# SSM parameters taken 128 channels at a time beside the units, half-height generator products, and a different opening

## The chip, the cores and the metric

The kernel runs on one core of a Trainium2 chip. A core has four engines that compute, each with its own instruction stream: TensorE (PE; its weight loads are listed as PEld), VectorE (DVE), ScalarE (ACT) and GpSimd (POOL). A fifth, SyncE (SP), issues nearly all DMAs here, one after the other in a fixed order. An engine works through its instructions in the order in which they were written and waits on semaphores for the others. The metric is the device time of one execution in microseconds (us). The kernel before took 719.56 us (median of three executions, 719.55 to 720.75).

## The reference

The input `x` is 2048 tokens of 640 channels. Two branches are mixed by a gate per token:

```
x = A_u
g = sigmoid((x * gate_w).sum(-1, keepdims=True))
a = S4D(x)                     # a long convolution per channel, plus u * D_skip
b = relu(x @ w1) @ w2          # 640 -> 1728 -> 640
out = g * a + (1 - g) * b

# S4D, per channel d, with N = 128 states:
dt = exp(log_dt);  A = -exp(log_A_real) + 1j * A_imag
C  = (C_real + 1j * C_imag) * dt[:, None]
P  = exp((A * dt[:, None])[:, :, None] * pos)      # 640 x 128 x 2048
K  = 2 * real(einsum("dn,dnl->dl", C, P))          # the taps, 640 x 2048
y  = irfft(rfft(u, 4096) * rfft(K, 4096))[:2048] + u * D_skip
```

## The kernel before, in words

The work has three strands, which share the engines.

**Feed-forward** (`feed_forward`). The 2048 tokens are 8 groups of 256, the 1728 hidden channels 14 blocks of 128, taken in three parts of 5, 5 and 4 blocks (`PARTS`). One group and one part are a unit: 75 matrix products for the hidden layer and 60 for the second layer (60 and 48 in the last part). Every operand is split into a high and a low half in a rounded 32-bit format, so each product is made three times (names `xh`, `xl`, `w1h`, `w1l`, `hh`, `hl`; output `pf`). In part 0 each group's input is transposed on TensorE (`pk<-ident,xs`), split by ScalarE and VectorE, and stored for the later parts.

**Parameters and taps** (`params`, `ssm`). `params` (L612 on) takes `log_A_real`, `A_imag`, `C_real`, `C_imag` and `log_dt` and makes, per channel and state, a phase step in turns, a decay exponent, the size of C and its angle. It does so with chains of VectorE steps on tiles of all 640 channels, 128 partitions by 5 x 128 columns: an exponential by polynomial (`exp_`, 13 steps), two reciprocals (five steps each), an arctangent and a square root on ScalarE, and some twenty steps that put the angle in the right octant. The results are split in high and low halves (`hl`) and written to a scratch in DRAM (`ps`), from which they are read back (`PS`) so that the eight rows of 16 channels lie over the 128 partitions.
`ssm` then makes the taps 16 channels at a time, 40 times. `phases(c)` multiplies the rows by a constant table `tg` on TensorE (`pg`, two products of 512 columns), ScalarE rounds (`cs<-pg`) and VectorE subtracts (`sn<-pg,cs`). `exponents(c)` makes decays the same way (`px`, two products; `pe`, one), ScalarE takes exponentials and sines, GpSimd scales by C (`cm`). `factors(c)` is five VectorE products (`G`, `mg`, `cs`, `sn`). For every two such pieces, `taps(p)` runs 128 small products (`pk`), VectorE turns the result (`kt`), GpSimd adds `D_skip`, and SP stores it (`kd`).

**Convolution** (`conv`). Five blocks of 128 channels, each a two-stage transform of the taps and of the input, a product in between and the two stages back: `stage1` (`pc<-ck,tf` and `pc<-ut,tf`), `stage2` (`pc<-vk,tm`, `pc<-va,tm`), `inv2` (`pc<-t,tn`), `relay` (VectorE transposes), `inv1` (`pc<-vk,tw`). `start` closes the memory of the taps and opens that of the convolution. The results meet the feed-forward sums there (`yj`) or in `feed_forward` (`with_y`, `with_last`).

**What sets the order.** Nothing is reordered on the chip. A planner (`Plan`) is given every piece of work as a task with its engine, an estimated duration, its dependences, the buffers it takes (rings) and a rank. It runs a model of the engines and, whenever an engine is free, writes out the ready task of lowest rank; the instruction streams have that order. All operations go through one helper, which is why nearly every row of the profile has the line L228: rows are told apart by the names of their tiles. In `params` every task has a rank of 3 or 4 behind the feed-forward tasks' 0, the loads of the parameters come after the last weights of part 0, and the memory of the parameters (`prm`) must be closed (`prm_shut`) before any phase product may start:

```
        opened = self.prm_shut = A('PY', 'open', 0, go, self.params())
        a = visit[c, 1] = A('PE', None, 0.5, pe, [rd, opened, *self.tg_done], take=[p_], use=[r_], rank=2, mode='f')
```

Of the kernel before, what the change touches and what calls it, by code (L numbers as in the profile page):

```python
# [10 lines left out]
F32 = mybir.dt.float32  # L11
# [13 lines left out]
BEHIND = 3  # L25
# [11 lines left out]
def tables():  # L37
# [23 lines left out]

    pt, mg, me = np.zeros((16, 8, 16, 64)), np.zeros((16, 8, 16, 64)), np.zeros((16, 8, 16, 32))
# [3 lines left out]
    tg = np.concatenate([x.reshape(128, -1) for x in (pt, mg, me)], axis=1)  # L66
# [183 lines left out]
class Kernel:  # L250
    def __init__(self, tc, ctx, io, out):
# [7 lines left out]
        self.sc = dict(kd=T([64, D, 32], "kd"), ps=[T([1, 128, 8, 128], "ps0"), T([NT - 1, 128, 8, 128], "ps1")],  # L259
# [18 lines left out]
    def feed_forward(self):  # L278
# [117 lines left out]
        def hidden(p, g, i, fs):  # L396
# [41 lines left out]
            a = A('ACT', 'ff', 0.12 + 0.2 * len(fs), high, ts, take=[h_], use=[b_], rank=0)  # L438
            b = A('DVE', 'ff', 0.08 + 0.27 * len(fs), low, [a], use=[b_, h_], rank=0)
            H[p, g, i] = (a, b), h_  # L440

        def sums(p, g, j, q_, qld):
# [35 lines left out]
            for k in range(0, 3 * n, 4 if j == 0 else 5):  # L478
# [6 lines left out]
                  use=[b_] if p == 0 and j == 0 else [b_, q_], rank=0)  # L485
# [61 lines left out]
        self.zst, self.x_read = [], []  # L547
        xs = {0: load_x(0)}
# [8 lines left out]
        for p, n in enumerate(PARTS):  # L557
            if p == 1:
                gates()
            for g in range(8):  # L560
# [11 lines left out]
                for k, i in enumerate(range(0, n, 2)):  # L572
                    hidden(p, g, i, range(i, min(i + 2, n)))
                    if nxt[0] == 0:
                        trans(g + 1, k, xs[g + 1])
                        if k == 2 and g < 6:
                            xs[g + 2] = load_x(g + 2)
# [11 lines left out]
                for t in range(2):  # L589
                    es = [sums(p, g, j, q_, mx[t]) for j in (2 * t, 2 * t + 1)]  # L590
# [21 lines left out]
    def params(self):  # L612
        tc, nc, io, A = self.tc, self.nc, self.io, self.plan.add
        V, S, D_ = self.V, self.S, self.D
        tl, last = {}, {}


        def step(eng, dur, fn, kb=0, ch='c', deps=()):
            last[ch] = [A(eng, 'prm' + ch, dur, fn, [*last[ch], *deps], kb=kb, rank=dict(a=4, c=3)[ch])]
            return last[ch][0]  # L620

        def start():
            pp = tl['pp'] = self.prm
            T = lambda n, d=F32: pp.tile([128, NT, 128], d, name=n)
            tl['dt'] = pp.tile([128, NT], F32, name="dt")
            D_.dma_start(tl['dt'], io['A_log_dt'].rearrange("(t p) -> p t", p=128))
            for k, n in (('la', "A_log_A_real"), ('ai', "A_A_imag"), ('cr', "A_C_real"), ('ci', "A_C_imag")):
                tl[k] = T(f"ld_{n}")
                D_.dma_start(tl[k], io[n].rearrange("(t p) n -> p t n", p=128))
            for n in ("th", "ac", "as", "mx", "mn", "r", "s", "ph", "ra", "sa"):  # L630
                tl[n] = T(n)
            tl['ni'] = T("ni", I32)
        self.prm_load = A('SP', 'prm', 3.1, start, kb=1300, rank=0)
        last.update(a=[self.prm_load], c=[self.prm_load])

# [5 lines left out]

        def split(r, src, ch):
            def high():
                tl['hl', r] = tl['pp'].tile([128, NT, 2, 128], F32R, name=f"hl{r}")
                S.copy(tl['hl', r][:, :, 0], tl[src])
            step('ACT', 0.75, high, ch=ch)
            step('DVE', 0.85, lambda: V.tensor_sub(tl['hl', r][:, :, 1], tl[src], tl['hl', r][:, :, 0].bitcast(F32)), ch=ch)
            for k, ts in enumerate((slice(0, 1), slice(1, NT))):
                rs = (4, 6) if r == 4 else (r,)

                def store(k=k, ts=ts, rs=rs):
                    for x in rs:
                        D_.dma_start(self.sc['ps'][k].rearrange("t p k n -> p t k n")[:, :, x:x + 2],
                                     tl['hl', r][:, ts].bitcast(F32))
                self.rows_st[k].append(A('SP', 'prm', 0.62 * len(rs), store, last[ch], kb=128 * (1, NT - 1)[k] * len(rs),
                                         rank=1))
        self.rows_st = [], []

        def exp_dt(V):
            small = [tl['pp'].tile([128, NT], d, name=f"sm{i}") for i, d in enumerate((I32, F32, F32))]  # L660
            exp_(V, tl['dt'], *small)
        steps(13, 0.18, exp_dt, 'a')
        dt = last['a']
        steps(13, 0.68, lambda V: exp_(V, tl['la'], tl['ni'], tl['ra'], tl['sa']), 'a')

        def scaled(V):
            for t in range(NT):
                d = tl['dt'][:, t:t + 1]
                V.tensor_scalar(tl['th'][:, t], tl['ai'][:, t], d, 1.0 / TWO_PI, op0=ALU.mult, op1=ALU.mult)
            for t in range(NT):  # L670
                d = tl['dt'][:, t:t + 1]
                V.tensor_scalar(tl['la'][:, t], tl['la'][:, t], d, -1.0, op0=ALU.mult, op1=ALU.mult)
        steps(2 * NT, 0.2, scaled, 'a')
        th = last['a']
        split(0, 'th', 'a')
        split(4, 'la', 'a')
        T_ = lambda: (tl[k] for k in ('ac', 'as', 'cr', 'ci', 'mx', 'mn', 'r', 's', 'ph', 'th', 'ni'))
        W = lambda f: (lambda: f(*T_()))
        R = lambda f: (lambda V: f(V, *T_()))

        step('ACT', 1.5, W(lambda ac, as_, cr, ci, *o: (S.activation(ac, cr, AF.Abs), S.activation(as_, ci, AF.Abs))))
        steps(3, 0.7, R(lambda V, ac, as_, cr, ci, mx, mn, r, *o: (
            V.tensor_tensor(mx, ac, as_, op=ALU.max), V.tensor_tensor(mn, ac, as_, op=ALU.min),
            V.tensor_scalar(r, mx, 1e-37, None, op0=ALU.max))))
        for t in range(NT):
            steps(1, 0.85, R(lambda V, ac, as_, cr, ci, mx, mn, r, s, *o, t=t: V.reciprocal(s[:, t], r[:, t])))
        steps(1, 0.75, R(lambda V, ac, as_, cr, ci, mx, mn, r, s, *o: V.tensor_mul(r, mn, s)))
        step('ACT', 2.8, W(lambda ac, as_, cr, ci, mx, mn, r, s, ph, *o: (
            S.activation(ph, r, AF.Arctan), S.activation(r, r, AF.Square))))
        steps(1, 0.45, R(lambda V, ac, as_, cr, ci, mx, mn, r, *o: V.tensor_scalar(r, r, 1.0, None, op0=ALU.add)))  # L690
        step('ACT', 2.1, W(lambda ac, as_, cr, ci, mx, mn, r, s, *o: S.activation(s, r, AF.Sqrt)))
        for t in range(NT):
            steps(1, 0.85, R(lambda V, ac, as_, cr, ci, mx, mn, r, s, *o, t=t: V.reciprocal(mn[:, t], s[:, t])))
        steps(3, 0.8, R(lambda V, ac, as_, cr, ci, mx, mn, r, s, *o: (
            V.tensor_mul(r, r, mn), V.tensor_add(s, s, r), V.tensor_mul(mx, mx, s))))

        def by_dt(V):
            for t in range(NT):
                V.tensor_scalar(tl['mx'][:, t], tl['mx'][:, t], tl['dt'][:, t:t + 1], None, op0=ALU.mult)
        steps(NT, 0.22, by_dt, deps=dt)  # L700
        steps(1, 0.45, R(lambda V, ac, as_, cr, ci, mx, mn, r, s, ph, *o: V.tensor_scalar(ph, ph, 1.0 / TWO_PI, None,
                                                                                         op0=ALU.mult)))
        for cond, two, turn in ((ALU.is_gt, True, 0.25), (ALU.is_lt, False, 0.5)):
            steps(4, 0.65, R(lambda V, ac, as_, cr, ci, mx, mn, r, s, ph, *o, cond=cond, two=two, turn=turn: (
                V.tensor_tensor(mn, as_, ac, op=cond) if two else V.tensor_scalar(mn, cr, 0.0, None, op0=cond),
                V.tensor_scalar(r, ph, -2.0, turn, op0=ALU.mult, op1=ALU.add),
                V.tensor_mul(r, r, mn), V.tensor_add(ph, ph, r))))
        steps(3, 0.6, R(lambda V, ac, as_, cr, ci, mx, mn, r, s, ph, *o: (
            V.tensor_scalar(mn, ci, 0.0, None, op0=ALU.is_lt),
            V.tensor_scalar(mn, mn, -2.0, 1.0, op0=ALU.mult, op1=ALU.add), V.tensor_mul(ph, ph, mn))))  # L710

        steps(3, 0.7, R(lambda V, ac, as_, cr, ci, mx, mn, r, s, ph, th, ni: (
            V.tensor_scalar(ni, th, 1008.0, None, op0=ALU.mult),
            V.scalar_tensor_tensor(r, th, 1008.0, ni, op0=ALU.mult, op1=ALU.subtract), V.tensor_add(ph, ph, r))), deps=th)
        split(2, 'ph', 'c')
        done = [*last['a'], *last['c'], *self.rows_st[0], *self.rows_st[1]]
        self.tg_done, tok = [], self.plan.token
        self.plan.ring('tgs', 2)
        for h in range(5):
            s_ = tok('tgs')  # L720
# [21 lines left out]
    def ssm(self, C=16):  # L742
# [32 lines left out]
        def load_rows(c):  # L775
            r_ = tok('PS')

            def load():
# [3 lines left out]
                for k in range(8):  # L782
                    R[c + k] = t[:, k]
# [425 lines left out]
```

## Time and profile before

| | |
|---|---|
| median of three executions | 719.56 us |
| the profiled execution | 716.08 us, of which span 714.3 us |
| PE busy | 672.8 us (94%) |
| DVE busy | 574.4 us (80%) |
| ACT busy | 389.2 us (54%) |
| POOL busy | 71.4 us (10%) |
| DMA | 110.83 MB, 155 GB/s over the span |

The profile is of one execution. The span runs from its first to its last instruction, and all times inside it count from its start. A row of a group of instructions reads: line, engine, operation, output <- inputs, partitions x elements, count, then busy time in us and the mean duration of one in ns, then the idle time of the engine before them and what ended it. Rows of a timeline read: start, duration, engine, line, operation, tiles, count. Busy times of one engine overlap at the seams, since an instruction may start before the last one's end is written; a busy TensorE need not be at its peak.

### The profile page before, as it was taken

The numbers are of one execution on the slowest core, as the hardware profiler recorded it, in microseconds if no ns is written. First come the engines' busy times: TensorE is split into PE (matmuls) and PEld (weight loads), VectorE is DVE, ScalarE is ACT, GpSimd is POOL, SyncE is SP. The second block draws the span as 40 slices with busy tenths as digits, with TensorE's granted clock in tenths as the row PEclk, the third lists the DMA queues.
The fourth block names the chain that finished last, engine by engine and source line by source line (L and its number), as shares of the span: only waits on it lengthen the run. The fifth ranks groups of instructions, "written<-read, shape, count | busy, mean of one in ns | idle before, by whom it ended". The sixth has DMA issues, their size and how long they took to land.

```text
span 714.3 us, 21601 instructions
## 1 busy us (share of the span) xinstructions
PE 672.8 (94%) x9469; PEld 594.5 (83%) x9469; DVE 574.4 (80%) x833; ACT 389.2 (54%) x572; POOL 71.4 (10%) x81
## 2 busy tenths in 40 slices
PE   5989999999999999999999999999699999699897
PEld 4989999889898899999999998887297587487695
DVE  4689628989999999999999873667969879479675
ACT  4353339989888978878888720134151341241330
POOL 1000002111122211122111100000000000010020
PEclk9999999999999999999999999999999999899999
DMA  8963764334556424423422659951643924731534
GB/s 202 260 236 137 272 207 148 86 124 164 164 206 225 146 93 140 160 68 132 160 93 91 235 198 315 290 180 50 140 109 119 225 76 161 139 88 56 121 97 96
DMA packets 92005, 110.83 MB, mean 155 GB/s; under 512 B 30912, under 2 KB 73416, under 8 KB 91656
## 3 DMA queue, kind: packets, MB, share of 16 engines
q1 hardware_dynamic: 91912, 109.46, 51.2%
q8 instruction: 74, 1.21, 0.7%
q14 instruction: 19, 0.16, 0.1%
HBM read 70.24 MB, written 39.20 MB: 153 GB/s over the span
## 4 chain that ended last, share of the span: by engine, by line
PE 69%; DVE 16%; ACT 8%; issue 2%; DMA 2%; SPq 2%; POOLq 0%; DVEq 0%; ACTq 0%
PE pf L228 42%; PE pc L228 18%; PE pk L228 5%; DVE sn L228 3%; ACT cs L228 2%; DVE vk L228 2%; PE pg L228 2%; DVE G L228 2%; DVE mg L228 2%; SPq L228 2%; PE px L228 1%; DVE cs L228 1%; DVE hl L228 1%; ACT L228 1%; ACT sn L228 1%
## 5 line engine op out<-in xcount | busy, mean ns | idle before, releaser
L228 PE MATMUL pf<-xh,w1h 128*128 128x256 f32 x560 | 163.3, 292 | 0.3 <-DVE hl L228 0.3
L228 PE MATMUL pf<-xl,w1h 128*128 128x256 f32 x560 | 160.4, 287 | 0.4 <-DVE xl L228 0.4
L228 PE MATMUL pf<-xh,w1l 128*128 128x256 f32 x560 | 159.9, 285 | 0.0
L228 PE MATMUL pf<-w2h,hh 128*128 128x320 f32 x448 | 140.4, 316 | 3.9 <-DVE hl L228 3.2
L228 PE MATMUL pf<-w2l,hh 128*128 128x320 f32 x448 | 137.9, 311 | 0.0
L228 PE MATMUL pf<-w2h,hl 128*128 128x320 f32 x448 | 126.8, 312 | 0.8 <-DVE hl L228 0.8
L228 PEld LDWEIGHTS pf<-xh,w1h 128*128 128x128 f32 x560 | 109.1, 195 | 6.7 <-issue 4.2
L228 PEld LDWEIGHTS pf<-xl,w1h 128*128 128x128 f32 x560 | 109.2, 195 | 1.6 <-DVE xl L228 0.7
L228 PEld LDWEIGHTS pf<-xh,w1l 128*128 128x128 f32 x560 | 109.3, 195 | 0.0
L228 ACT ACTIVATE hh<-pf 128x512 fp32r<-128x512 f32 (+1 forms) x64 | 34.8, 543 | 127.7 <-PE pf L228 122.0
L228 PEld LDWEIGHTS pf<-w2h,hh 128*128 128x128 f32 x448 | 84.1, 188 | 16.3 <-issue 7.2
L228 PEld LDWEIGHTS pf<-w2l,hh 128*128 128x128 f32 x448 | 84.2, 188 | 5.5 <-issue 4.9
L228 DVE TENSOR_TENSOR t<-pc,kw 128x512 f32<-128x512 f32 x80 | 53.8, 691 | 42.0 <-ACT kw L228 42.0
L228 PEld LDWEIGHTS pf<-w2h,hl 128*128 128x128 f32 x448 | 80.7, 188 | 8.3 <-issue 5.9
L228 POOL TENSOR_TENSOR me<-me,cm 128x512 f32<-128x512 f32 x40 | 50.5, 1262 | 182.3 <-DVE cs L228 103.9
L228 DVE TENSOR_TENSOR mg<-mg,cs 128x1024 f32<-128x1024 f32 x40 | 58.2, 1454 | 1.1
L228 DVE SCALAR_TENSOR_TENSOR hl<-pf,hh 128x512 fp32r<-128x512 f32 (+1 forms) x64 | 39.7, 623 | 20.4 <-ACT hh L228 20.2
L228 ACT COPY kw<-pc 128x256 f32<-128x256 f32 x80 | 29.7, 373 | 47.5 <-PE pc L228 44.9
L228 ACT ACT_TABLE_LOAD x42 | 53.9, 1283 | 0.8
L228 DVE TENSOR_TENSOR sn<-pg,cs 128x1024 f32<-128x1024 f32 x40 | 48.7, 1218 | 6.5 <-ACT cs L228 6.0
L228 PE MATMUL pc<-va,tm 64*64 64x128 f32 x1280 | 53.4, 275 | 0.0
L228 ACT CAST cs<-pg 128x1024 int32<-128x1024 f32 x40 | 40.4, 1010 | 22.0 <-PE pg L228 21.8
(138 smaller groups left out, 1221.5 us busy)
## 6 DMA issues: line engine op xcount, KB each, us to landing
part<-q SPq DMA_DIRECT2D x16, 640.0 KB, 3.8
xh<-xt SPq DMA_DIRECT2D x16, 640.0 KB, 6.6
xl<-xt SPq DMA_DIRECT2D x16, 640.0 KB, 5.2
q<-part SPq DMA_DIRECT2D x16, 640.0 KB, 4.1
ws<-in_B_w_dram SPq DMA_DIRECT2D x22, 320.0 KB, 3.5
xs<-in_A_u_dram SPq DMA_DIRECT2D x16, 320.0 KB, 4.0
xt<-xh SPq DMA_DIRECT2D x8, 640.0 KB
xt<-xl SPq DMA_DIRECT2D x8, 640.0 KB
```

The lines of the kernel that those rows point to most:

```text
L228: return lambda *a, **k: self._tc.keep_in_program_order(f(*a, **k))
```

## The change

The parameters are made in five passes of 128 channels (`params(t)`), each on tiles of 128 x 128, in one set of buffers that the passes share. Pass 0 stands in front, at rank 3. The others have rank 0.8 (`PRM`), that is ahead of the tasks of the taps, and each load waits for the end of the pass before; from the third pass on it also waits for a point seven pieces ahead (`AHEAD`) of the first piece that needs it. Each pass has its own scratch (`ps`), its own transposition of the scale (`cm`), and the rows are read back 64 channels at a time. Memory for tables is opened and closed apart from that for the parameters, so that phase products wait for the tables and their own pass only.

The tables of phases and of coarse decays keep the part that 8 channels need, twice, over partitions 0 to 63 and 64 to 127. A phase product of 128 rows and 512 columns becomes one of 64 rows and 512 columns, on the upper or the lower half of TensorE's rows; the number of products is the same. The fine decays (`pe`) stay whole. The table shrinks from 2560 to 1536 columns, three loads and casts instead of five.

Ten products of the identity with itself are put first on TensorE (`SPIN`). The convolution's first table (`tf`) is loaded in the feed-forward's opening, and the convolution's memory opens on the last addition of `D_skip`, no longer on the taps' stores. The last unit's output is stored in four smaller pieces, one of them issued by ScalarE. The order of two tasks in the transposition of the input is written more generally, with the same result for these parts, and `LOW` and `YIELD` are in place with an empty range.

```diff
+SPIN = 10
+PRM = 0.8
+AHEAD = 7
...
-    tg = np.concatenate([x.reshape(128, -1) for x in (pt, mg, me)], axis=1)
+    tg = np.concatenate([np.tile(x[:8, :, :8].reshape(64, -1), (2, 1)) for x in (pt, mg)] + [me.reshape(128, -1)], axis=1)
...
+        def spin():
+            p = self.psg.tile([128, 16, 32], F32, name="pe").rearrange("p a b -> p (a b)")
+            for _ in range(SPIN):
+                self.E.matmul(p[:, :128], self.ident, self.ident, start=True, stop=True)
+        if SPIN:
+            A('PE', 'ff', 1.7 + 0.43 * SPIN, spin, mode='f')
...
+                    if g == 7 and t and to == D:
+                        es = [sums(p, g, 2, q_, mx[t])]
+                        wl = with_last(g, t, q_, mx[t])
...
+                        A('SP', 'st', 1.24, out(0, (0, 1), D_), es, use=[q_], kb=160, rank=6)
+                        es = [sums(p, g, 3, q_, [*mx[t], wl])]
+                        ds.append(A('SP', 'st', 0.62, out(320, (0,), D_), es, use=[q_], kb=80, rank=6))
+                        ds.append(A('ACT', 'st', 0.62, out(320, (1,), S), es, use=[q_], kb=80, rank=6))
...
-    def params(self):
+    def params(self, t):
...
+        def step(eng, dur, fn, ch='c', deps=(), mode=None):
+            last[ch] = [A(eng, 'prm' + ch, dur, fn, [*last[ch], *deps], rank=PRM if t else 3, mode=mode)]
+            return last[ch]
+
+        def load():
+            for k, n in (('la', "A_log_A_real"), ('ai', "A_A_imag"), ('cr', "A_C_real"), ('ci', "A_C_imag")):
+                D_.dma_start(tl[k], io[n][t * 128:t * 128 + 128])
+        ld = A('SP', 'prm', 2.5, load, [*self.prm_end, *([self.prm_dt] if t == 0 else [])], kb=256, rank=0 if t == 0 else 3)
...
-        steps(13, 0.68, lambda V: exp_(V, tl['la'], tl['ni'], tl['ra'], tl['sa']), 'a')
+        steps(13, 0.22, lambda V: exp_(V, tl['la'], tl['ni'], tl['ra'], tl['sa']), 'a')
...
+        a = A('PE', 'cm', 0.3, cm_pe, last['c'], take=[p_], rank=1.5, mode='f')
...
+        self.prm_end = [*last['a'], *last['c'], *rows, a]
...
-        opened = self.prm_shut = A('PY', 'open', 0, go, self.params())
+        opened = self.prm_shut = A('PY', 'open', 0, go, self.tg_done)
+        for t in range(NT):
+            self.params(t)
...
-                t = gk.tile([128, 8, 128], F32R, name="PS", bufs=2)
+                t = gk.tile([128, 4, 128], F32R, name="PS", bufs=2)
...
                 for h in range(2):
-                    x = slice(h * 512, h * 512 + 512)
-                    self.E.matmul(pf[:, x], R[c], self.tg[:, x], start=True, stop=True)
+                    r = slice(64 * h, 64 * h + 64)
+                    self.E.matmul(pf[:, h * 512:h * 512 + 512], R[c][r], self.tg[r, :512], start=True, stop=True)
...
+                    self.E.matmul(pf[:, h * 512:h * 512 + 512], R[c][r], self.tg[r, 512:1024], start=True, stop=True)
+                self.E.matmul(q.rearrange("p d j -> p (d j)"), R[c], self.tg[:, 1024:], start=True, stop=True)
...
+        for t in range(1, NT):
+            if 8 * t - 8 >= AHEAD:
+                self.prm_load[t].deps += (tasks[8 * t - 8 - AHEAD]['abs'],)
...
-        opened = self.opened = A('PY', 'open', 0, start, self.kd.values())
+        opened = self.opened = A('PY', 'open', 0, start, [self.kd_out])
...
-        tf = table('tf', [128, 2, 128], 't_f1')
+        def load_tf():
+            st['tf'] = self.early.tile([128, 2, 128], F32, name="tf")
+            D_.dma_start(st['tf'], io['t_f1'])
+        tf = A('SP', 'tab0', 0.62, load_tf, kb=128, rank=6)
...
-        self.prm_load.deps += (self.wload[0, PARTS[0] - 1, 1],)
+        self.prm_dt.deps += (self.wload[0, 0, 0],)
         self.prm_shut.deps += tuple(self.w_first)
         for x in self.late_loads:
-            x.deps += (self.wload[0, PARTS[0] - 1, 1],)
+            x.deps += (self.wload[0, PARTS[0] - 1, 0],)
```

More of the change, by code (lines that the diff above doesn't have):

```diff
@@ L574, in feed_forward @@
                     if nxt[0] == 0:
[L575 to L576 removed]
+                        for third in range(k, 3 if i + 2 >= n else k + 1):
+                            trans(g + 1, third, xs[g + 1])
+                        if i + 2 >= n and g < 6:
                             xs[g + 2] = load_x(g + 2)
@@ L639, in steps @@
                 step('DVE', dur, rec.one(k, n, lambda: fn(rec)), ch=ch, deps=deps if k == 0 else ())
+        rows = self.rows_st[t] = []
         def split(r, src, ch):
[L643 to L647, printed above, removed]
@@ L673, in params, with store @@
-        steps(2 * NT, 0.2, scaled, 'a')
+            step('ACT', 0.24, lambda: S.copy(tl['hl', r][:, 0], tl[src]), ch=ch, deps=rows[:1] if r == 2 else ())
+            step('DVE', 0.24, lambda: V.tensor_sub(tl['hl', r][:, 1], tl[src], tl['hl', r][:, 0].bitcast(F32)), ch=ch)
+            rs = (4, 6) if r == 4 else (r,)
+            def store():
+                for x in rs:
+                    D_.dma_start(self.sc['ps'][t][:, x:x + 2], tl['hl', r].bitcast(F32))
+            rows.append(A('SP', 'prm', 0.62 * len(rs), store, last[ch], kb=128 * len(rs), rank=1))
@@ L674, in params @@
         th = last['a']
-        split(0, 'th', 'a')
+        split(0, 'ai', 'a')
         split(4, 'la', 'a')
[L677 to L707, printed above, removed]
@@ L732, in cm_pe @@
         def cm_pe():
             px = self.psg.tile([128, 4, 256], F32, name="px")
-            tl['pe'] = px.rearrange("p a b -> p (a b)")[:, :D].rearrange("p (t d) -> p t d", d=128)
-            for t in range(NT):
-                self.E.transpose(tl['pe'][:, t], tl['mx'][:, t], self.ident)
-        a = A('PE', 'cm', 1.1, cm_pe, last['c'], take=[p_], rank=2, mode='f')
-        self.cm_done = A('ACT', 'cm', 1.2, lambda: S.copy(self.cm[:].rearrange("p (t d) -> p t d", d=128), tl['pe']), [a],
-                         use=[p_], rank=1)
```

174 lines of the change are left out of this document (92 added, 82 removed).

## The prediction

> **What bounds the kernel now.** I read the stage windows first, then the chain of work that ended last, then the groups of instructions. The windows are cut at the first sine factor (103.3 us from the span's start), the last turn of the taps (423.8), the start of convolution block 0's second stage (470.7) and the end of that block (513.5); columns are the stretch and its length, then busy time of each engine with its instruction count.
>
> ```profile
> core 0: us, PE busy (x) PEld busy (x) DVE busy (x) ACT busy (x) POOL busy (x), PEclk, DMA share, GB/s
> 80.00:100.00 20.00, 20.00 (x156) 19.95 (x155) 3.76 (x7) 4.69 (x11) 0.00 (x0) 1.00 0.99 319
> ...
> 103.30:423.80 320.50, 311.62 (x4420) 292.72 (x4419) 299.53 (x415) 269.85 (x322) 59.09 (x59) 1.00 0.43 142
> 200.00:400.00 200.00, 196.46 (x2824) 184.44 (x2823) 192.66 (x272) 168.54 (x192) 40.48 (x40) 1.00 0.40 134
> 423.80:470.70 46.90, 46.65 (x347) 39.27 (x350) 24.26 (x34) 4.96 (x8) 0.21 (x1) 1.00 0.97 287
> 470.70:513.50 42.80, 37.61 (x779) 28.42 (x779) 33.35 (x42) 14.32 (x30) 0.00 (x0) 1.00 0.34 107
> 513.50:714.30 200.80, 186.02 (x3284) 144.56 (x3284) 151.76 (x223) 59.85 (x140) 10.25 (x12) 0.98 0.48 118
> ...
> PE 69%; DVE 16%; ACT 8%; issue 2%; DMA 2%; SPq 2%; POOLq 0%; DVEq 0%; ACTq 0%
> ```
>
> TensorE alone would seem the bound (94% of the span, 69% of the chain). The stage decides otherwise. In the 320.5 us in which the taps are made, VectorE is busy 299.5 and TensorE 311.6; at 200 to 400 they stand at 96.3% and 98.2%. Both are full at once, so work added to either lengthens this stage. VectorE's large free stretch lies before it: 3.76 busy of the 20 us at 80 to 100.
>
> The next rows count the feed-forward products (pf), which fill TensorE between the other work; one unit of 256 tokens and one part of the hidden channels has 135.
>
> ```profile
> core 0: us, PE busy (x) PEld busy (x) DVE busy (x) ACT busy (x), PEclk, DMA share, GB/s
> 0.00:61.02 61.02, 45.12 (x299) 43.88 (x300) 4.45 (x8) 6.58 (x14) 0.94 0.80 237
> ...
> 102.49:423.80 321.31, 229.97 (x1639) 220.79 (x1638) 38.55 (x72) 26.22 (x53) 1.00 0.43 142
> 423.80:470.70 46.90, 39.21 (x279) 37.17 (x278) 8.98 (x16) 2.39 (x4) 1.00 0.97 287
> 470.70:513.50 42.80, 10.22 (x69) 9.03 (x69) 1.38 (x2) 1.20 (x2) 1.00 0.34 107
> ...
> 409.95 11.79 PE pf L228 x90
> ```
>
> A pf product costs 11.79 / 90 = 0.131 us on the chain.
>
> **The change, part by part.** The orders in which both kernels' instructions stand on each engine give the frame. Before: the first phase product stands behind 585 pf, the last tap product behind 2220, block 0's second stage behind 2499. After: 300, 2345, 2544. From the end of block 0 on (2568 in both) TensorE's order is the same product for product. So I sum four pieces: the start of the taps stage, its length, the way to block 0's end, the rest.
>
> *Start.* Only the first 128 channels' parameters are now in front.
>
> ```profile
> 102.60 0.63 PE L228 MATMUL pg<-tg,PS 128*128 128x512 f32 x2
> 103.07 0.63 PE L228 MATMUL px<-tg,PS 128*128 128x512 f32 x2
> 103.54 0.39 PE L228 MATMUL pe<-tg,PS 128*128 128x512 f32 x1
> 103.77 0.28 PE L228 MATMUL pf<-xh,w1h 128*128 128x256 f32 x1
> ...
> 104.32 1.22 DVE L228 TENSOR_TENSOR sn<-pg,cs 128x1024 f32<-128x1024 f32 x1 [1.30 <-ACT cs L228]
> ...
> 79.12 0.82 DVE L228 TENSOR_TENSOR hl<-ld_A_log_A_real,hl 128x640 fp32r<-128x640 f32 x1
> ...
> 90.50 3.02 SPq L228 DMA_DIRECT2D PS<-ps  x2
> ```
>
> The 300th pf product started at 61.0 before, and 1.7 us lie between a phase product and its sine factor (102.60 to 104.32). If the first rows are ready, VectorE starts the stage at 61.0 + 1.7 = 62.7 instead of 104.3: 42 us earlier.
>
> *VectorE's new work.* This is the price that decides. Per 128 channels there are 44 steps: 26 with two inputs, 16 with one, 2 reciprocals.
>
> ```profile
> L228 DVE SCALAR_TENSOR_TENSOR sa<-sa,ra 128x640 f32<-128x640 f32 x6 | 4.9, 820 | 0.1
> L228 DVE TENSOR_SCALAR r<-mx 128x640 f32<-128x640 f32 x1 | 0.5, 487 | 0.0
> L228 DVE SCALAR_TENSOR_TENSOR sm<-sm,sm 128x5 f32<-128x5 f32 x6 | 1.0, 165 | 0.2
> L228 DVE TENSOR_SCALAR th<-ld_A_A_imag,dt 128x128 f32<-128x128 f32 x5 | 1.1, 283 | 0.0
> L228 DVE RECIPROCAL mn<-s 128x128 f32<-128x128 f32 x5 | 4.3, 914 | 0.0
> ...
> 40.28 0.83 DVE L228 SCALAR_TENSOR_TENSOR ra<-ni,ld_A_log_A_real 128x640 f32<-128x640 int32 x1
> 41.14 0.83 DVE L228 SCALAR_TENSOR_TENSOR ra<-ni,ra 128x640 f32<-128x640 int32 x1
> ```
>
> A step of 5 columns takes 0.165 and one of 640 takes 0.82 to 0.83 with two inputs, 0.487 with one. In a straight line, 128 columns take 0.165 + 0.66 x 123/635 = 0.29 and 0.23. The steps form a chain, and one that needs the last one's result starts 0.86 after it (40.28 to 41.14), 0.03 over its duration; so 0.33 and 0.26. A group costs 26 x 0.33 + 16 x 0.26 + 2 x 0.88 (0.914 less the overlap of neighbours) = 14.5. Four of five groups fall into the full stage: 58 us that stood before it. Bounds: where neighbours do not depend, five steps take 1.07 (0.21 each), a group 42 x 0.21 + 1.7 = 10.5; with 0.34 for all, 16. I take 14.5, since each step reads the one before and the order keeps them together.
>
> [...]
>
> Feed-forward work moves too: 2345 - 300 = 2045 pf now lie in the stage, not 1635. 410 more are 3.0 units; one costs VectorE the 3.76 us that the 80 to 100 window shows: 11 us.
>
> *Length.* VectorE: 299.5 + 58 + 11 = 368.5 busy. At the 96.3% of the 200 to 400 window that is 383 us, and the last turn comes at 62.7 + 383 = 445.7, 22 us later than before. TensorE: 311.6 + 410 x 0.131 = 53.7, less what the row tiles save. The two phase products start 0.47 apart from the next pair, the decays too; halves of 64 rows that run side by side would save 0.235 twice per 16 channels, 40 x 0.47 = 18.8. That leaves 346.5, and without any overlap of the halves 365: both under 383. So the saving turns into idle time of TensorE, and 0 of it reaches the end. ScalarE: 10 more table loads in its order at 1.28, some 36 small steps at 0.3, three units at 4.69: 269.9 + 13 + 11 + 14 = 308, also under.
>
> ```profile
> L228 ACT ACT_TABLE_LOAD x42 | 53.9, 1283 | 0.8
> ...
> 428.38 0.59 SPq L228 DMA_DIRECT2D ut<-in_A_u_dram  x1
> ...
> 432.49 2.01 SPq L228 DMA_DIRECT2D tf<-in_t_f_dram  x1
> ...
> ut<-in_A_u_dram SPq DMA_DIRECT2D x10, 512.0 KB, 9.7
> ...
> 707.15 4.35 SPq L228 DMA_DIRECT2D out_dram<-q  x4
> ```
>
> *To the end of block 0.* From the last turn to the second stage 199 pf stand instead of 279: 46.9 - 80 x 0.131 = 36.4. The first table (tf, 2.0 us of SP's queue here) is loaded early and the input (ut) no longer waits for the taps' stores; but ut's products now stand behind only some 91 pf (12 us) and ut needs about 4 us to its issue and 9.7 to land, so I add 1: 37.4. In block 0 only 24 pf stand instead of 69; VectorE works 33 of the 43 us there, and TensorE's 45 fewer products lie in its shadow. I take 1 off: 41.8 (bounds 37 and 42.8).
>
> *The rest.* Same order, 200.8. The last store leaves in pieces, one by ScalarE's queue: one issue of four in 4.35 less, near half hidden: -0.6.
>
> *The head.* Ten identity products run before the first input lands.
>
> ```profile
> 19.24 0.69 DVE L228 TENSOR_TENSOR xl<-pk,xh 128x512 fp32r<-128x512 f32 x1
> ...
> 13.14 0.41 PE L228 MATMUL pf<-xh,w1l 128*128 128x256 f32 x1
> ...
> 14.19 0.28 PE L228 MATMUL pf<-xh,w1l 128*128 128x256 f32 x1
> ...
> 17.35 1.09 PE L228 MATMUL pk<-ident,xs 128*128 128x128 f32 x4 [2.17 <-DMA xs<-in_A_u_dram]
> ...
> 18.45 0.41 PE L228 MATMUL pf<-xl,w1h 128*128 128x256 f32 x1
> ```
>
> Products are slow (0.41 at 13.1), fast (0.28) just after, then TensorE waits 2.17 for the second input, after which they are slow again. Faster first products only lengthen that wait, so I count 0. [...] Two fewer table loads and casts for the generator (five become three) lie under this stretch as well. SP carries 16 more parameter loads and some 10 more row stores and loads; at 0.3 to 1.2 us an issue they lie in a queue that mostly waits, but a store of rows now holds back what stands behind it.
>
> *Sum.* 445.7 + 37.4 + 41.8 + 200.8 - 0.6 = 725.1 against 714.3: +10.8. The profiled execution took 716.08, so 726.9; the median of the runs shown is 719.56, 3.5 above it, so 730.4 there. I say 730. A measurement here tells about 0.2% (1.4 us) from no change.
>
> **Rivals.** (1) Not slower: the parameter steps overlap as independent ones. At 10.5 a group the stage has 352.5 of VectorE, ends at 62.7 + 366 = 428.7, and the kernel takes 713.4. It decides at 12.0 a group, 0.27 a step. For it: 0.21 in the scaling rows. Against it: those five do not depend on each other.
> (2) TensorE sets the stage's length, because VectorE runs nearly without a gap (98%, as TensorE does now) and at the lower price: 346.5 / 0.972 = 356.5 (its present 311.6 of 320.5), the last turn at 419.2, 704 in all. Against it: VectorE's sum, even at 10.5 a group and with 98% of the time, is 360. [...]
> (3) The early start does not come about. Before, the first phase product followed the last parameter row (79.12 + 0.82) by 22.7 us, because SP stands in line: the rows were loaded at 90.5. The first group's last row should be ready near 49: after the second input's low part (19.24) VectorE's order holds a group (14.5), 13 steps for the time constants at 0.2 and some 6 us of feed-forward, and the chain goes to ScalarE and back three times, about 2 us each with the table loads. With the same delay the stage starts at 71.7 + 1.7, 10.7 later, and 741 results. From 61 - 49 = 12 us of delay on it costs one for one. Against it: fewer stores stand between.
> (4) The gain and the loss cancel within 1.4.
>
> **How the numbers follow.** Forecast 0.55, (3) 0.15, (1) 0.16, (2) 0.08, (4) 0.06. (1) and (2) make faster 0.24, (4) same 0.06, the others slower 0.70. The range runs from just under (1), 712, to (3), 741: it leaves out (2) and the far end of (3). Where it is slower, I expect 724 to 738.
>
> **What would show it.** Right: the first pg near 61, the last kt near 446, VectorE above 95% busy between, TensorE with some 35 us idle there, parameter steps of 128 columns near 0.29 starting 0.33 apart, and about 243 us from block 0's second stage to the end. Wrong: steps starting 0.21 apart; the last kt before 435; a first pg after 70; or a second half that isn't the same although its order is.

## The result and the profile after

The changed kernel takes 729.12 us (median of four executions, 727.41 to 730.23), against 719.55 (714.72 to 720.75) for the kernel before on the same chip. The two medians are 1.3% apart; the ratio on record is 1.0159, 95% interval 1.0134 to 1.0184. It is slower. The profiled execution took 727.41 us, its span 725.6, 11.3 more than the span before.

Stage windows of the changed kernel, cut at the end of the head, the last turn of the taps, the start of block 0's second stage and the end of that block (columns as in the prediction's windows):

```profile
core 0: us, PE busy (x) PEld busy (x) DVE busy (x) ACT busy (x) POOL busy (x), PEclk, DMA share, GB/s
0.00:61.00 61.00, 51.36 (x361) 49.55 (x361) 30.94 (x87) 25.88 (x51) 1.81 (x9) 0.94 0.81 236
61.00:445.40 384.40, 367.23 (x4853) 334.73 (x4852) 358.24 (x613) 304.25 (x394) 58.19 (x59) 1.00 0.46 151
445.40:479.70 34.30, 34.30 (x263) 28.15 (x263) 21.13 (x27) 1.79 (x3) 0.21 (x1) 1.00 0.98 253
479.70:525.00 45.30, 36.18 (x737) 25.32 (x736) 33.50 (x44) 13.88 (x29) 0.00 (x0) 0.89 0.38 124
525.00:725.60 200.60, 184.54 (x3283) 142.98 (x3280) 151.17 (x221) 59.85 (x140) 10.16 (x12) 0.98 0.48 118
```

The kernel before, in the windows that answer to these up to the taps' end:

```profile
0.00:61.00 61.00, 49.31 (x329) 48.32 (x330) 41.67 (x78) 26.80 (x46) 1.81 (x9) 0.94 0.80 237
61.00:423.80 362.80, 353.25 (x4739) 333.96 (x4738) 323.32 (x460) 283.28 (x349) 59.09 (x59) 1.00 0.46 150
```

TensorE's work hardly changed, 672.8 us before and 673.6 after, so the 11.3 us are almost all idle time of TensorE, and subtracting its busy time from each window says where it arose. Head: 11.7 before, 9.6 after. From 61 us to the last turn: 9.6 and 17.2. Way to block 0: 0.2 and 0. Block 0: 42.80 - 37.61 = 5.2 and 9.1. The rest: 14.8 and 16.1. So the long stage holds 7.6 us more of this idle time and block 0 3.9, the head 2.1 less. Where idle time lies is not yet what caused it.

The next rows show the two prices that mattered, those of a half-height pair and of a parameter step: a row of the kernel before (the product ahead of the unit whose rows stand in the prediction), TensorE's timeline around a unit of the changed kernel, two of its weight loads, and a view of tiles (duration as shortest/median/longest).

```profile
102.49 0.28 PE L228 MATMUL pf<-xh,w1l 128*128 128x256 f32 x1
```

```profile
148.13 0.28 PE L233 MATMUL pf<-xh,w1l 128*128 128x256 f32 x1
148.33 0.50 PE L233 MATMUL pg<-tg,PS 64*128 64x512 f32 x2
148.67 0.39 PE L233 MATMUL px<-tg,PS 64*128 64x512 f32 x2
148.99 0.50 PE L233 MATMUL pe<-tg,PS 128*128 128x512 f32 x1
149.33 0.28 PE L233 MATMUL pf<-xh,w1h 128*128 128x256 f32 x1
...
148.33 0.19 PEld L233 LDWEIGHTS pg<-tg,PS 64*128 64x128 f32 x2
148.99 0.19 PEld L233 LDWEIGHTS pe<-tg,PS 128*128 128x128 f32 x1 [0.36 <-issue]
```

```profile
L233 DVE SCALAR_TENSOR_TENSOR p_sa<-p_sa,p_ra x30: 283/292/294, 30.5 to 249.2; 128x128 f32<-128x128 f32 x30
L233 DVE TENSOR_SCALAR p_sa<-p_ra x5: 227/228/1110, 30.3 to 246.4; 128x128 f32<-128x128 f32 x5
L233 DVE TENSOR_TENSOR p_mx<-p_mx,p_s x5: 291/291/1156, 39.4 to 262.4; 128x128 f32<-128x128 f32 x5
```

The five products of a unit now start 0.34, 0.32 and 0.34 us apart (two, two, one), 1.00 in all, where before five times 0.23 made 1.16. But the first pair also starts later behind the product ahead of it, 0.20 us where it was 0.11. From that product to the one behind the unit it is 1.20 now and was 1.28; by the medians over all units of the traces 1.21 and 1.28, a gain of 0.07. The steps' durations are the 0.29 and 0.23 that were read off before, but for a few of over 1 us.

### The profile page after: what moved, and what is told of

It is laid out like the page before. It is cut to its first block, busy times and chain, and to the rows that moved or that the text cites. A ratio compares the mean times of both kernels' runs of the same rounds, so it can differ in the third digit from the quotient of the medians.

```text
span 725.6 us, 21881 instructions
## 1 busy us (share of the span) xinstructions
PE 673.6 (93%) x9489; PEld 580.7 (80%) x9489; DVE 595.0 (82%) x989; ACT 405.7 (56%) x616; POOL 70.4 (10%) x81
## 3 DMA queue, kind: packets, MB, share of 16 engines
q8 instruction: 74, 1.21, 0.7%
## 4 chain that ended last, share of the span: by engine, by line
PE 63%; DVE 22%; ACT 6%; issue 5%; DMA 3%; SPq 1%; DVEq 0%; ACTq 0%
PE pf L233 36%; PE pc L233 19%; PE pk L233 4%; DVE sn L233 3%; DVE mg L233 2%; DVE G L233 2%; DVE cs L233 2%; DVE p_sa L233 2%; DVE hl L233 2%; PE pg L233 1%; PE pe L233 1%; ACT cs L233 1%; ACT L233 1%; DMA tgs<-in_t_g_dram 1%; DVE yj L233 1%
## 5 line engine op out<-in xcount | busy, mean ns | idle before, releaser
L233 DVE TENSOR_TENSOR t<-pc,kw 128x512 f32<-128x512 f32 x80 | 54.0, 691 | 46.4 <-ACT kw L233 46.3
L233 PE MATMUL pc<-t,tn 64*64 64x128 f32 x1280 | 46.2, 276 | 4.7 <-issue 3.6
```

What stands on the lines that cost most here:

```text
L233: return lambda *a, **k: self._tc.keep_in_program_order(f(*a, **k))
```

## The experiments

A ratio is to the kernel before, run beside each; the changed kernel's is 1.0159.

**More work for TensorE, less for VectorE.** Three kernels ask which of the two sets the stage's length.

```
e1: both products of a pair on the upper half
-                    r = slice(64 * h, 64 * h + 64)
+                    r = slice(0, 64)
e4: phase pair twice
-                for h in range(2):
+                for h in (0, 1, 0, 1):
e3: fewer steps in passes 1 to 4
-        steps(12, 0.21, octants)
+        if t == 0:
+            steps(12, 0.21, octants)
...
-    for k in (720, 120, 24, 6, 2, 1):
+    for k in (720, 120, 24, 6, 2, 1) if whole else ():
```

> The changed kernel, but both products of each pair of phases and of coarse decays use the upper 64 rows, so that they run one after the other. Instruction order as in the changed kernel; the second half's phases and decays are wrong (it uses the first half's rows), so the values of the taps are. Theory V (VectorE alone sets the length of the stage in which the taps are made): TensorE gains 80 x about 0.13 us = 10 us of work there and has 17 us idle, so the time stays at 729, within 2.5. Theory T (TensorE, at 367 of 384 us, sets it as well): about 10 us longer, 739. Theory B (each waits for the other in turn): 3 to 6 us longer.

> The changed kernel with each pair of phase products issued twice (the same result): 80 more matrix products, 40 pairs of 0.33 us = 13 us of TensorE's work in the stage, nothing more on VectorE. Theory V: 729 to 731, TensorE's 17 us of idle time takes it. Theory T: 13 us longer, 742. Theory B: 5 to 8 us longer.

> The changed kernel with 18 of the 44 VectorE steps left out in the second to fifth group of channels (the six of the exponential's polynomial, the twelve of the octants), 72 steps in all; the decays and phases of these channels are wrong. At the 0.25 to 0.33 us spacing measured after the change this is 18 to 24, about 21 us of VectorE's work. Theory V: 20 us faster than the changed kernel, until TensorE's 367 bounds the stage: between 709 and 713, which is faster than the kernel before. Theory T: within 3 us of 729. Theory B: about half, 718 to 722.

Measured: one half 741.86 us (1.0339, 1.0282 to 1.0397), phase pair twice 729.66 (1.0170, 1.0133 to 1.0207), fewer steps 712.12 (0.9928, 0.9899 to 0.9956). From first sine factor to last turn, the three in this order:

```profile
61.90:459.70 397.80, 385.90 (x4851) 350.21 (x4849) 359.12 (x612) 305.41 (x393) 57.98 (x59) 0.99 0.45 146
```

```profile
61.10:447.80 386.70, 374.73 (x4927) 340.64 (x4925) 358.55 (x612) 304.51 (x393) 57.87 (x59) 1.00 0.46 150
```

```profile
62.00:425.90 363.90, 349.19 (x4726) 317.52 (x4725) 338.59 (x533) 294.17 (x383) 57.48 (x59) 1.00 0.46 150
```

With 72 steps fewer VectorE is busy 338.6, 19.7 less, and the stage ends 20 us sooner; the kernel is even faster than before. The planner also moved 121 feed-forward products behind the stage, so TensorE has less to do in it; but over the whole span TensorE's work is the changed kernel's (674.4 us against 673.6), and the 17 us that are gained come from VectorE's steps. (The moved products make the way from the last turn to the end 6.5 us longer.) With 7.5 us more on TensorE (374.7 against 367.2) the stage grows by some 2 to 3 and the time by nothing that can be told. With 18.7 more it grows by 14. So VectorE sets the length of the changed kernel's stage, and TensorE stands so close behind that it takes over after some 5 us. The increments are not those that the expectations gave: a phase pair issued right behind another costs 0.22 us and not 0.33, and the serial pairs cost 0.47 a unit. Both say the same: two halves side by side take just the time of one (in the changed kernel's trace the second starts 3 ns behind the first, by the median), and the rest of the 0.33 belongs to the change of height in front of them or behind them.

**Parts of the change on the kernel before.**

```
e2, e6, e11: half-height pairs and the small table as in the change; planned durations
e2: 0.3 and 0.55 (as in the change)     e6, e11: 0.5 and 0.7 (as before)
e11 besides: tf early, opened = A('PY', 'open', 0, start, [self.kd_out]), last store in pieces
```

> The kernel before with one part of the change alone: phases and coarse decays as pairs of products of 64 rows, with the table of 1536 columns in place of 2560 (three loads and casts in place of five). All 128 channels' parameters still stand ahead. Measured in the changed kernel, a unit of 16 channels has its products shortened by 0.17 us, not the 0.47 that I took: 40 units, 7 us. Theory T: 7 us faster, 712 to 713. Theory V: at most 2 us faster (two table pieces fewer), 717 to 720. If the overlap were whole after all: 19 us, about 701.

> The kernel before with the half-height pairs, as in the run with that part alone, but with the planner told the old durations (0.5 and 0.7 us), so that TensorE and VectorE have exactly the order of the kernel before; only the products' height and two table pieces differ. Theory R (the reordering made that run 5 us slower): 710 to 717, the 7 us of TensorE's work gained in part or not at all. Theory S (the switches of shape themselves cost it): 721 to 724 again.

> The kernel before with all of the change but the two parts at the front: the half-height pairs (planned durations as before), the first table loaded early, the convolution opened by the last tap and not by its stores, the last store in pieces. All parameters of 640 channels stand ahead, and there are no identity products. If the loss comes from the parameters beside the units, this is as fast as the half-height pairs alone or faster: 711 to 716. My prediction's steps for the way to block 0 and its end would give 5 to 10 less than 716. If these parts cost as well: 718 or more.

Measured: 722.40 us (1.0070, 1.0046 to 1.0094) with the shorter planned durations, 715.88 (0.9970, 0.9946 to 0.9994) with the old ones, 714.10 (0.9953, 0.9927 to 0.9980) with the rest of the change too. The first two issue the same work on VectorE and TensorE; one has 78 more feed-forward products in front of the last turn (the 2299th stands there instead of the 2221st), and takes 6.5 us longer. The first was slower than any of its expectations. So what the half-height pairs and the small table gain with the order kept is 0.3%, and the planner's new order had taken that and more. The third beats both kernels: it has everything but the parameters beside the units, the identity products and the shorter planned durations of the pairs, and gains 3.3 us on the kernel before; the changed kernel is 15 behind it. No run divides these 15 among the three. On the kernel before the planned durations alone were worth 6.5, the next run gives the identity products up to 4, and the run with fewer steps shows that 72 of the 176 parameter steps in the stage cost 17 in the changed kernel. The intervals of the second and the third overlap, so the early table's share is not told apart from nothing. The 5 to 10 us expected of it did not come: block 0's second stage starts 33.6 us after the last turn and not 46.8, but with 93 feed-forward products fewer in front of it (2406 against 2499), which follow later.

**The identity products.**

```
-SPIN = 10
+SPIN = 0
```

> The changed kernel without the ten identity products at the head. My forecast counted them at nothing, since faster first products only lengthen TensorE's wait for the second input: within 1.5 of 729. Rival: they bring the clock up earlier and save what the slow products cost, so the time grows by about 2 without them, 731. A third: they only stand in front, and 1 to 2 us are gained by leaving them out, 727.

Measured: 725.13 us (1.0103, 1.0061 to 1.0145), 0.0056 below the changed kernel's ratio, 4 us. The intervals overlap a little, so a small loss through the identity products is likely and its size open; none of the three expectations is right within its margin. In the profiles the 30th feed-forward product starts at 15.46 us without them and 12.99 with them, the 60th at 23.51 and 23.81: what is won at the head is lost in the wait for the second input. Where the 4 us would come from is not shown.

**The steps on another engine.** GpSimd is busy 58 us in the stage.

```
e8: pool=(0, 2, 3, 4, 6, 7, 8, 10, 11) of the octants, pool=range(4, 17) of the exponential
e9, e12: also both scalings, the low halves, six steps of the angle and the size, one of the last three
+                g = t and k in pool
+                step('POOL' if g else 'DVE', 0.4 if g else dur, one, ...)      # e12: 0.62 and dur + 0.08
```

> The changed kernel with 16 of the 44 parameter steps of each of the last four groups moved from VectorE to GpSimd (nine octant steps; the exponential's polynomial, where seven steps of VectorE become thirteen of GpSimd), nothing left out. GpSimd is busy 58 of the stage's 384 us. 64 steps at 0.27 are 17 us less on VectorE. Theory V: 15 to 18 faster than the changed kernel, 711 to 715, and so faster than the kernel before. Rival P (GpSimd's steps hold VectorE up in the same time, or their greater length delays the rows): 722 to 730.

> As the run before it, with 28 of the 44 steps of each of the last four groups on GpSimd: 112 steps at 0.27, 30 us less on VectorE. Theory V with TensorE next: the gain flattens where TensorE, full at about 97%, becomes the bound; 704 to 710. If VectorE alone counted: 699. Rival P: 722 or more.

> The run with 28 of 44 steps on GpSimd again, with the planner told 0.62 us for a step there (measured 0.43 to 1.07) and 0.08 more for those that stay on VectorE. That run's stage lasted 374.8 us where VectorE's 336 / 0.935 and TensorE's 350 / 0.97 both give 360: 14 us of waits behind GpSimd. If these come from steps planned too short, 712 to 718; if GpSimd's slowness and its hold on VectorE remain, 724 to 730.

Measured: 742.94 us (1.0340, 1.0296 to 1.0385), 728.12 (1.0139, 1.0096 to 1.0181), 726.21 (1.0136, 1.0080 to 1.0193): the rival, and the first beyond it. Groups of the second of the three, on GpSimd and on VectorE:

```profile
L237 POOL TENSOR_SCALAR p_sa<-p_sa 128x128 f32<-128x128 f32 x24 | 14.6, 606 | 2.1
L237 POOL TENSOR_TENSOR p_sa<-p_sa,p_ra 128x128 f32<-128x128 f32 x24 | 11.3, 469 | 2.0
...
L237 POOL TENSOR_SCALAR p_mx<-p_mx,dt 128x128 f32<-128x128 f32 x4 | 4.3, 1074 | 0.3
...
L237 DVE TENSOR_SCALAR cs<-sn 128x1024 int32<-128x1024 int32 x40 | 31.8, 796 | 0.8
```

A wait of the same kernel (in all, times, longest, us) and its stage:

```profile
DVE p_la L237 <- POOL p_sa L237: 10.5, 4, 3.4
```

```profile
61.10:435.90 374.80, 349.96 (x4722) 316.74 (x4721) 336.10 (x494) 294.35 (x383) 137.57 (x195) 0.99 0.45 145
```

VectorE has 22 us less to do and TensorE 17 (125 feed-forward products stand behind the stage instead of in it), but the stage shrinks by 9 only, and those products make the time behind it 8 longer. A step costs mostly 0.47 to 1.07 us on GpSimd, VectorE waits 10.5 us in four places for the chain to come back, and its own rounding step (`cs<-sn`) takes 0.80 on average where its median is 0.69. Longer planned durations changed the time by 2 us, within the intervals. Why the first of the three, with fewer steps moved, is the slowest stays open.

**The planned durations of the steps.**

```
-        steps(13, 0.22, lambda V: exp_(V, tl['la'], ...
+        steps(13, 0.31, lambda V: exp_(V, tl['la'], ...
...                                                       # and so for the other steps
```

> The changed kernel with one thing different: the planner is told durations near the measured ones for the parameter steps (0.31 and 0.25 us, 0.95 for a reciprocal, in place of 0.2 to 0.22 and 0.35), so that its order gives these steps the room that they take. Theory V with the reading of the runs so far (the stage lasts VectorE's busy time / 0.935 or TensorE's / 0.97, whichever is longer): no work goes, so within 3 us of 729. Theory R (an order planned with too short steps is what costs): 5 or more faster, 724 or less.

Measured: 744.96 us (1.0408, 1.0380 to 1.0436), 16 us slower, which neither theory had. The stage, 50 us inside it, and the two stretches behind it, with all work and then with the feed-forward products alone:

```profile
62.60:462.00 399.40, 382.64 (x4946) 349.58 (x4945) 360.72 (x619) 306.98 (x396) 58.00 (x59) 0.98 0.47 153
200.00:250.00 50.00, 41.66 (x606) 35.90 (x605) 46.03 (x76) 35.70 (x43) 9.57 (x9) 0.90 0.51 163
462.00:495.00 33.00, 21.70 (x155) 14.94 (x156) 15.88 (x19) 2.75 (x4) 0.21 (x1) 0.84 1.00 265
495.00:535.00 40.00, 29.55 (x696) 22.52 (x696) 27.67 (x34) 10.66 (x24) 0.00 (x0) 0.80 0.22 49
```

```profile
62.60:462.00 399.40, 303.47 (x2141) 291.78 (x2142) 51.41 (x94) 35.09 (x71) 0.98 0.47 153
495.00:535.00 40.00, 0.00 (x0) 0.00 (x0) 0.00 (x0) 0.00 (x0) 0.80 0.22 49
```

The planner, seeing longer gaps, put 95 more feed-forward products into the stage (2141 against 2046) and 27 more ahead of it. The stage grew by some 15 us. By the table below TensorE is the bound there (394); besides, at 200 to 250 it was idle for 8.3 us, where VectorE was busy 46.0 of 50. Behind the stage nothing was gained for it. Few products were left there and none in block 0, TensorE was idle for 11 and 10 us at a granted clock of 0.84 and 0.80, and from the last turn to the end it takes 281.1 us (743.1 - 462.0) against 280.2. No engine had been given more work. What moved was the filler.

**One reading of all runs.** Before, VectorE was busy 299.53 of the stage's 320.5 us (93.5%) and TensorE 311.62 (97.2%). If each engine reaches that share and no more, the stage lasts the longer of two quotients, worked out here from each run's stage window. Two windows that are not shown above are those of the half-height pairs alone, with shorter and with old planned durations:

```profile
104.20:432.00 327.80, 316.75 (x4492) 286.20 (x4491) 303.49 (x420) 270.62 (x323) 60.46 (x59) 1.00 0.45 146
106.10:423.30 317.20, 306.55 (x4414) 275.97 (x4413) 299.01 (x415) 268.77 (x321) 59.25 (x59) 1.00 0.44 144
```

| kernel | VectorE / 0.935 | TensorE / 0.972 | stage |
|---|---|---|---|
| changed | 383 | 378 | 384 |
| one half | 384 | 397 | 398 |
| phase pair twice | 383 | 386 | 387 |
| fewer steps | 362 | 359 | 364 |
| no identity products | 383 | 379 | 386 |
| planner told | 386 | 394 | 399 |
| pairs alone, shorter planned | 325 | 326 | 328 |
| pairs alone, old planned | 320 | 315 | 317 |
| the rest | 320 | 317 | 319 |
| 16 steps on GpSimd | 371 | 380 | 391 |
| 28 steps on GpSimd | 359 | 360 | 375 |
| 28 steps, longer planned | 361 | 367 | 373 |

Six of the twelve lie up to 3 us above the longer quotient, the run with the planner told 6 above. The two that keep the order of the kernel before lie 3 and 1 below it: VectorE reached 94.3 and 93.8% there, so its share is no ceiling. The three with steps on GpSimd lie 6 to 15 above, with the waits that this added. It is a reading of twelve runs, not a law; the rows for one half and for the phase pair are what supports it most, since there the order stayed and TensorE's work alone was changed.

## Why the prediction came out right, step by step

The span was forecast at 725.1 and is 725.6. Most of the places hold: the first phase product at 59.56 (61 forecast), the first sine factor at 61.72 (62.7), the last turn at 445.4 (445.7), the rest 200.6 (200.2). So rival (3), a late start, is out. But two steps behind the 445.7 were wrong and cancelled: that the last turn came out to 0.3 us is luck. What holds is the mechanism, a start some 42 us earlier and a stage that grows by more than that because VectorE is full.

*VectorE's work* (forecast 368.5, measured 358.2). Without the parameter steps VectorE is busy for 309.2 us of the stage in the trace. So the three units, with all else that moved, cost 9.6 (11 forecast) and the four groups of steps 49, 12.3 a group and not 14.5. The durations were right, and so was the distance where a step needs the result of the one before: 0.33 with two inputs, 0.25 with one. What failed is "each step reads the one before it". Of the 148 places in the stage where such a step follows another, 56 have starts only 0.13 to 0.21 apart, shorter than the first step lasts; these are places where the second does not need the first. Besides, the 0.03 between dependent steps is idle time, and I had put it into busy time. On price rival (1) was nearer: VectorE's 358.2 is what the sum has at the 12.0 a group from which it was to decide (299.5 + 11 + 48 = 358.5).

*The share* (forecast 96.3%, measured 358.24 / 384.4 = 93.2%). I took it from the best 200 us of the stage. The quoted row of the whole stage said 93.5%, and by it 358.2 gives 383. Rival (1) failed on this: it reckoned with the same 96.3%. The run with fewer steps shows that the direction was right all the same: with 19.7 us less for VectorE the stage is 20 us shorter.

*TensorE's idle time* (forecast 35 us, measured 17). This is the step that failed outright, and with it "the saving turns into idle time". The term for the row tiles, 18.8, measured 0.07 x 40 = 2.9: the two halves of a pair do run side by side, but each change of height costs time. The run with the pairs alone and the old order agrees: over its span TensorE is busy 669.4 us, 3.4 less than before. And a feed-forward product costs more in the stage than the 0.131 of the chain:

```profile
61.00:445.40 384.40, 288.53 (x2046) 276.45 (x2047) 47.69 (x88) 33.84 (x69) 1.00 0.46 151
```

288.53 - 229.97 for 407 more products is 0.144 each, 58.6 in all and not 53.7. With 346.5 + 15.9 + 4.9 = 367.3 the two make up all that was missing (367.2 measured). What I left out is a price for the change of height. The rows show it: the second half starts 3 to 4 ns behind the first, and four starts in a unit come about 0.10 later than in the kernel before, two at each change. The first pair starts 0.09 later behind the product ahead of it, and the next pair 0.10 later behind it; the whole product starts 0.09 later, and the product behind it 0.11. That is 0.39 of the 0.47 that the overlap saves. Had TensorE been as idle as I said, the run with one half would not have become 13 us slower. Rival (2) is out all the same, but by 5 us (378 against 383) and not by the forecast's 26.

*Block 0* (forecast 37.4 to its second stage and 41.8 for it, measured 34.3 and 45.3; that the sum is right is luck). I gave fewer fillers no price, inside bounds of 37 to 42.8, and 45.3 lies outside them. With 25 products instead of 69 TensorE stands still twice. The first two rows are windows of the kernel before and the next two of the changed one, cut at the first transposition between the stages (`vk<-va`); the rest is the changed kernel's timeline:

```profile
470.70:491.80 21.10, 21.09 (x663) 18.80 (x664) 11.65 (x18) 13.12 (x28) 0.00 (x0) 1.00 0.29 95
491.80:513.50 21.70, 16.51 (x117) 9.61 (x116) 21.70 (x26) 1.20 (x2) 0.00 (x0) 1.00 0.38 119
...
479.70:504.50 24.80, 21.98 (x658) 19.94 (x658) 13.39 (x21) 12.81 (x28) 0.00 (x0) 0.93 0.51 175
504.50:525.00 20.50, 14.20 (x80) 5.37 (x79) 20.11 (x25) 1.07 (x2) 0.00 (x0) 0.83 0.23 63
...
492.84 0.71 PE L233 MATMUL pc<-t,tn 64*64 64x128 f32 x13 [2.44 <-issue]
508.92 1.09 PE L233 MATMUL pc<-ck,tf 64*64 64x512 f32 x8
515.11 1.98 PE L233 MATMUL pc<-ck,tf 64*64 64x512 f32 x8 [4.62 <-issue]
...
504.50 8.76 DVE L233 STREAM_TRANSPOSE vk<-va 128x512 f32<-128x512 f32 x8
513.17 3.59 DVE L233 STREAM_TRANSPOSE vk<-pc 128x512 f32<-128x512 f32 x4
```

The longer stop is not the costly one. In the second part of the block VectorE works almost without a gap in both kernels, and that part is even 1.2 us shorter than before. There TensorE waits for VectorE, which has eight transpositions to do before those that free TensorE's buffers (`pc`, three of them): in the trace the wait ends at 515.06 on VectorE's semaphore, 0.05 after the second of these, while the taps' rows (`ck`) had landed by 507.6. After 4.62 us without work the same eight products take 1.98 instead of 1.09. The granted clock was 1.00 in the first case (508.0 to 510.0 us) and 0.50 in the second (515.1 to 517.1). VectorE loses 0.4 us by it (20.11 busy of the part's 20.50).

The block lost its time in the first part, 24.8 us against 21.1. There TensorE stopped for 2.44 us in the middle of a group of 32 products, at a place for which the trace has no wait, and the granted clock of the part fell to 0.93. Three more runs with this order of products have such a stop there (2.44, 3.81 and 2.11 us in one half, phase pair twice and no identity products); the kernel before has none over 0.9 in the block. What causes it stays open. Fewer fillers as such are not the reason: the run with the planner told has none in the block, and it takes 45.6 us from its second stage to that of the next block, where the changed kernel takes 48.1 and the kernel before 46.4.

*The head* was counted at nothing, and its products started earlier and waited longer, as said; leaving them out may gain up to 4 us.

## What to carry to other kernels

Where several engines are nearly full in a stage, write down for each its busy time over the share that it reaches in the whole stage, not in the best part of it, and take the longest; an engine that seems to gain slack may be 5 us behind. Where low-priority work fills the gaps, its total does not change, so ask where each piece of it stands after the change: too much in a full stage lengthens it, and taking it out of a stage that another engine fills may gain nothing there. And a price taken as a distance from start to start holds the gaps already; dividing it by a share of busy time counts them twice.

## What was not expected of the hardware

Half-height products beside whole ones cost two changes of height a unit here, about 0.2 us each by the medians over the units: 0.09 ahead of the first product of the new height and 0.10 behind it. The weight loads show what the second half of this is. In the unit shown the weights of the second pair are loaded 0.23 us ahead of it, while the first pair runs, and those of the feed-forward product ahead of the unit 0.12 ahead (148.01 for 148.13); but the first product behind a change starts together with its own load: 148.33 and 148.33 for the pair, 148.99 and 148.99 for the whole product. A pair between pairs (phase pair twice) takes 0.22 and a whole product among whole ones 0.23.

VectorE steps are now and then held for almost the length of a GpSimd multiplication: `p_sa<-p_ra` takes 0.23 us, and 1.11 at the longest, while GpSimd's `me<-me,cm` takes 1.23 on average, 1.05 in half of its cases and mostly 1.5 in the others:

```profile
L233 POOL TENSOR_TENSOR me<-me,cm 128x512 f32<-128x512 f32 x40 | 49.4, 1234 | 174.2 <-ACT me L233 96.0 <-DVE p_ra L233 70.7 <-DMA ps<-hl 5.2
...
147.48 0.69 DVE L233 TENSOR_TENSOR G<-mg,sn 128x512 f32<-128x512 f32 x1
147.58 1.50 POOL L233 TENSOR_TENSOR me<-me,cm 128x512 f32<-128x512 f32 x1
...
246.40 1.05 POOL L233 TENSOR_TENSOR me<-me,cm 128x512 f32<-128x512 f32 x1 [9.36 <-DVE p_ra L233]
246.42 1.11 DVE L233 TENSOR_SCALAR p_sa<-p_ra 128x128 f32<-128x128 f32 x1
```

Which of the two is held depends in these rows on which started first. All seven parameter steps that started while a multiplication ran were held and took 0.96 to 1.16 instead of 0.23 to 0.29, some 5.6 us in all. Of the 15 `G<-mg,sn` (TENSOR_TENSOR) that lie mostly under a multiplication, 14 had started before it: they took 0.68 to 0.70, as elsewhere, and it was the multiplication that took longer. The one that started during it took 1.54. The steps `sn<-pg,cs`, which read TensorE's output, were not held: 12 of them, mostly under a multiplication, took 1.21, and the others 1.22. Why the one kind is held and the other not is not shown.
